# Two x batches and the later states transposed by DMA, a reordered dual phase, and a later softmax in an attention and maxout kernel

## Chip, cores and metric

One core of one Trainium2 chip. The metric is device time in microseconds (us) of one launch, lower is better. A run more than 1.5% above the fastest of the same kernel counts as slow. The kernel before takes 166.33 us (median of 4 runs, 166.04 to 167.13).

## The reference, cut

For each of 8 batches and 8 heads, x (512 x 64) and a state (32 x 64) read each other by softmax attention. The results are laid side by side into 4352 tokens of 512 features and go through a maxout layer and an output layer:

```python
scores = scale * x @ state.T;  xread = softmax(scores) @ state
scores2 = scale * state @ x.T; sread = softmax(scores2) @ x
x = concat([xread, sread], axis=2)          # -> (8 * 544, 512)
h = maximum(maximum(x @ w1, x @ w2), x @ w3)  # 512 -> 768
out = h @ w_out                              # 768 -> 512
```

## The kernel before

The kernel never forms xread. It folds the states into the weights once per batch (G = state times w1, w2, w3) and multiplies the transposed attention weights (aT) with G: "maxout" below, six matmuls of 512 columns for one of six column blocks, evacuated by one copy on ScalarE and two maxima on VectorE. The order of each engine's instructions is the program order. Batches 0 and 1 run together in a "dual phase"; from batch 2 on there is a loop, in which batch n = b + 1 is prepared in slots between the six maxouts of batch b.

```python
def load_x(b):                       # float32 in HBM -> bf16, cast by the DMA, GpSimd queue
    nc.gpsimd.dma_start(out=x_sb[b]..., in_=x[b]...)

def states(k, copy):                 # states of batches 2k, 2k+1
    p = pp.tile([128, 4, 128], BF16, tag="pw", bufs=4, name="pt")
    for t in range(4):
        nc.tensor.transpose(p[:, t, :], st[k][:, t]..., ident)
    for c in range(2):
        copy(out=bds[k][...], in_=p[...])

def x_transpose_dma(b):
    new(xT, b, [128, H, 2, 128], "xT")
    nc.sync.dma_start_transpose(out=xT[b]..., in_=x_sb[b][:, 0:XW])

def a_transpose_dma(b):
    new(aT, b, [128, J, 2, 128], "aT", bufs=3)
    nc.sync.dma_start_transpose(out=aT[b]..., in_=a[b]...)

# ... end of the dual phase, cut
    states(1, dve)
    x_transpose(2, 0, dve); x_transpose(2, 1, dve)      # on TensorE
    x_maxout(1, 3)
    g_cols(0, (5,), defer=both)
    scores(2, 0, 2); softmax(2, 0, 2, nc.gpsimd.tensor_mul)
    # ...
    a_transpose(2, 0, act); a_transpose(2, 1, dve)      # on TensorE
    ffn_out(0, 0); g_cols(2, (2, 3)); ffn_out(0, 1); g_cols(2, (4, 5))

for b in range(2, B):                                   # cut
    n = b + 1
    if n == 3: slots[0] += x_transpose(n, ...)          # on TensorE
    slots[0 or 1] += scores(n), softmax(n)
    slots[2] += a_transpose_dma(n)
    slots[3] += sread(n), states((n + 1) // 2, act)
    # G pieces in slots 1 (2 for n = 3), 4, 5; output pieces of batch b - 1 in slots 1, 2, 4, 5
```

The softmax here doesn't subtract the row's maximum and nothing guards it: scores larger than these inputs give would overflow.

## Time and profile before

| | before |
|---|---|
| median of 4 runs | 166.33 us |
| span of the profiled run | 164.5 us |
| TensorE busy | 149.7 us, 91% |
| ScalarE, VectorE, GpSimd busy | 60%, 58%, 27% |
| granted TensorE clock | 1.0 throughout |

TensorE is the engine to watch: it is on 63% of the chain of waits (the work followed back from the last instruction, at each step to what released it), and the others have slack over the whole. The prediction shows the lines and reads them.

### The profile page before, as it was taken

The numbers are of one execution on the slowest core, as the hardware profiler recorded it, in microseconds if no ns is written. First come the engines' busy times: TensorE is split into PE (matmuls) and PEld (weight loads), VectorE is DVE, ScalarE is ACT, GpSimd is POOL, SyncE is SP. The second block draws the span as 40 slices with busy tenths as digits, with TensorE's granted clock in tenths as the row PEclk, the third lists the DMA queues.
The fourth block names the chain that finished last, engine by engine and source line by source line (L and its number), as shares of the span: only waits on it lengthen the run. The fifth ranks groups of instructions, "written<-read, shape, count | busy, mean of one in ns | idle before, by whom it ended". The sixth has DMA issues, their size and how long they took to land.

```text
span 164.5 us, 3569 instructions
## 1 busy us (share of the span) xinstructions
PE 149.7 (91%) x1432; PEld 70.9 (43%) x1449; DVE 96.0 (58%) x162; ACT 99.1 (60%) x158; POOL 44.0 (27%) x64
## 2 busy tenths in 40 slices
PE   7658699988999999999999999999999999999990
PEld 2425243533445444434344434444444466665430
DVE  4675777889418553665548464865586455585001
ACT  3355578366896678853876688648755853333440
POOL 8975550106150601081016101410141010100140
PEclk9999999999999999999999999999999999999999
DMA  4999999800039999269992989460306030030373
GB/s 132 195 174 199 204 200 248 122 7 0 0 120 130 144 256 198 53 116 145 277 193 87 133 187 104 162 191 14 128 0 195 8 130 0 0 132 0 128 235 148
DMA packets 31824, 20.94 MB, mean 127 GB/s; under 512 B 17184, under 2 KB 29344, under 8 KB 31808
## 3 DMA queue, kind: packets, MB, share of 16 engines
q0 software_dynamic: 15632, 15.08, 46.3%
q1 hardware_dynamic: 16176, 5.64, 18.5%
q8 instruction: 11, 0.18, 0.5%
q14 instruction: 5, 0.04, 0.1%
HBM read 15.20 MB, written 8.91 MB: 147 GB/s over the span
## 4 chain that ended last, share of the span: by engine, by line
PE 63%; DVE 11%; ACT 10%; DMA 6%; POOL 4%; issue 4%; DVEq 0%; ACTq 0%; POOLq 0%
PE pw L260 34%; PE po L285 20%; DMA x<-in_x_dram 4%; PE pg L239 4%; DVE den L183 4%; DVE t L267 3%; ACT e L176 3%; ACT G L245 3%; DVE ht L268 3%; PE ps L171 2%; ACT t L264 2%; PE psr L216 2%; POOL w L94 1%; DMA out_dram<-osb 1%; POOL a L186 1%
## 5 line engine op out<-in xcount | busy, mean ns | idle before, releaser
L260 PE MATMUL pw<-aT,G 128*128 128x512 bf16 x288 | 71.2, 379 | 3.6 <-ACT G L245 1.8
L267 DVE TENSOR_TENSOR t<-t,pw 128x512 bf16<-128x512 bf16 (+1 forms) x54 | 35.1, 650 | 41.6 <-ACT t L264 40.0
L285 PE MATMUL po<-wout,ht 128*128 128x512 bf16 x188 | 47.9, 380 | 0.8
L260 PEld LDWEIGHTS <-G 128*128 128x128 bf16 x288 | 26.7, 98 | 36.2 <-issue 5.1
L245 ACT CAST G<-pg 128x768 bf16<-128x768 f32 x48 | 36.5, 805 | 8.0 <-PE pg L239 7.6
L264 ACT CAST t<-pw 128x512 bf16<-128x512 f32 (+1 forms) x54 | 30.5, 566 | 14.1 <-PE pw L260 12.6
L268 DVE TENSOR_TENSOR ht<-t,pw 128x512 bf16<-128x512 bf16 (+1 forms) x54 | 35.5, 658 | 5.6
L292 ACT COPY osb<-po 128x512 f32<-128x512 f32 x33 | 19.4, 587 | 21.2 <-PE po L285 20.7
L285 PEld LDWEIGHTS <-ht 128*128 128x128 bf16 x204 | 18.4, 98 | 23.6 <-issue 4.7
L301 POOL DMA_DIRECT2D out_dram<-osb x14 | 7.8, 559 | 70.2 <-ACT osb L292 70.2
L186 POOL TENSOR_TENSOR a<-e,rden 128x1024 bf16<-128x1024 bf16 (+1 forms) x8 | 14.4, 1800 | 33.4 <-DVE rden L185 19.8
L239 PE MATMUL pg<-w,bd 64*32 64x384 bf16 x384 | 13.0, 328 | 1.1 <-DMA w<-in_moe_w_dram 1.1
L183 DVE TENSOR_REDUCE den<-e 128x32 f32<-128x1024 bf16 (+1 forms) x9 | 9.9, 1095 | 2.6 <-ACT e L176 2.6
L176 ACT ACTIVATE e<-ps 128x1024 bf16<-128x1024 f32 x7 | 7.2, 1024 | 5.8 <-PE ps L171 5.8
L260 PE MATMUL pw<-ats,w 128*128 128x256 bf16 x72 | 8.8, 273 | 0.0
L239 PEld LDWEIGHTS <-bd 64*32 64x32 bf16 x384 | 3.6, 89 | 11.7 <-issue 11.7
L260 PEld LDWEIGHTS <-w 128*128 128x128 bf16 x72 | 7.0, 98 | 2.1
L94 POOL DMA_DIRECT2D w<-in_moe_w_dram x9 | 6.8, 770 | 0.0
L69 POOL DMA_DIRECT2D x<-in_x_dram x7 | 6.7, 957 | 0.0
L150 PE MATMUL pxt<-ident,x 128*128 128x128 bf16 x64 | 4.4, 219 | 2.2 <-DMA x<-in_x_dram 1.1
L134 ACT COPY bd<-pt 64x512 bf16<-64x512 bf16 x6 | 3.5, 580 | 4.2 <-PE pt L131 4.1
L171 PEld LDWEIGHTS <-xT 128*128 128x128 bf16 x128 | 4.7, 98 | 2.4 <-DVE xT L153 0.8
(42 smaller groups left out, 63.4 us busy)
## 6 DMA issues: line engine op xcount, KB each, us to landing
out_dram<-osb POOLq DMA_DIRECT2D x14, 512.0 KB, 3.7
x<-in_x_dram POOLq DMA_DIRECT2D x7, 512.0 KB, 9.0
w<-in_moe_w_dram POOLq DMA_DIRECT2D x3, 384.0 KB, 10.3
w<-in_moe_w_dram POOLq DMA_DIRECT2D x3, 256.0 KB, 8.2
wout<-in_moe_w_out_dram POOLq DMA_DIRECT2D x1, 768.0 KB, 16.4
x0f<-in_x_dram SPq DMA_DIRECT2D x1, 512.0 KB, 4.0
out_dram<-osb SPq DMA_DIRECT2D x1, 512.0 KB, 2.7
out_dram<-osb SPq DMA_DIRECT2D x2, 256.0 KB, 2.2
```

What stands on the lines that cost most here:

```text
L94: nc.gpsimd.dma_start(out=w_sb[c][:, :, i, :], in_=w.rearrange("(kk p) f -> p kk f", p=128)[:, :, m0 * 128:m1 * 128])
L176: nc.scalar.activation(out=e[b][:, :, g0:g1], in_=p, func=AF.Exp, scale=scale)
L183: nc.vector.reduce_sum(out=den, in_=e[b][:, :, g0:g1], axis=AX.X)
L186: mul(out=a[b][:, :, g0:g1].rearrange("p j g s n -> p j (g s) n"), in0=e[b][:, :, g0:g1].rearrange("p j g s n -> p j (g s) n"), in1=rden.r ...
L239: nc.tensor.matmul(p[32 * s:32 * s + 32, g, 0:384].rearrange("p (i f) -> p i f", i=3), bd(b, 2 * s + g)[64 * g:64 * g + 64, g, :], w[64 * ...
L245: copy(out=G[b][:, :, m * 384:(m + 1) * 384], in_=p[:, :, 0:384])
L260: nc.tensor.matmul(p[:, 0:n], lhs(i, k), rhs(k), start=(k == 0), stop=(k == nk - 1))
L264: nc.scalar.copy(out=t0[:, 0:n], in_=pw[0][:, 0:n])
L267: nc.vector.tensor_max(t1[:, 0:n], t0[:, 0:n], pw[1][:, 0:n])
L268: nc.vector.tensor_max(ht[b][:, m, :], t1[:, 0:n], pw[2][:, 0:n])
L285: nc.tensor.matmul(p, ht[b][:, m, j * 128:(j + 1) * 128], wout_sb[:, m, :], start=(m == 0), stop=(m == NM - 1))
L292: nc.scalar.copy(out=o[:, j, :], in_=p)
```

## The change

The intent: take transposes off TensorE (x of batches 2 and 3, states of groups 1 to 3, a of batch 2) and give them to the DMA; place states with GpSimd in place of ScalarE and VectorE; finish batch 0 (its last output pieces too) inside the dual phase, with the G pieces in pairs; move the loop's softmax behind the next maxima; split the last store. The diff, cut to its core:

```diff
 def states(k, copy):
-    p = pp.tile(...); 4 x nc.tensor.transpose(...)
+    if k == 0: (as before)
+    else:
+        p = data.tile([128, 4, 128], BF16, name=f"stT{k}")
+        nc.sync.dma_start_transpose(out=p, in_=st[k]...)
 ...
+    load_st(1, nc.scalar)
 ...
+    states_cast(1, pool)
     ... load_x(3)
+    states(1, pool)
+    x_transpose_dma(2)
 ...
-    x_maxout(1, 1); g_cols(0, (3, 4)); ...; x_maxout(1, 2); x_maxout(0, 3)
+    x_maxout(1, 1); x_maxout(1, 2); g_cols(0, (4, 5), defer=both)
+    x_maxout(0, 3); x_maxout(0, 4); g_cols(1, (3, 4), defer=both)
+    x_maxout(0, 5); x_maxout(1, 3)
     scores(2, 0, 2)
     softmax(2, 0, 2, nc.gpsimd.tensor_mul)
+    a_transpose_dma(2)
+    x_transpose_dma(3)
+    load_x(4)
 ...
+    ffn_out(0, 0) ... ffn_out(0, 3)     # all four output pieces of batch 0
 for b in range(2, B):
-    slots[0] softmax(n); slots[3] states(.., act); slots[4] g_cols(n, (2, 3))
+    slots[1] softmax(n); slots[2] states(.., pool); slots[3] g_cols(n, (2, 3))
 # last output piece: two tiles, stored on ScalarE's and SyncE's queues
-    act(o[:, j, 0:256]); dve(o[:, j, 256:512]); one store
+    act(halves[0]); store; dve(halves[1]); store
```

More of the change, by code (lines that the diff above doesn't have):

```diff
@@ L53 @@
     ctx.enter_context(tc.manual_schedule())
+    dve, act, pool = nc.vector.tensor_copy, nc.scalar.copy, nc.gpsimd.tensor_copy
     def load_st(k, eng):
@@ L127, in states @@
     def states(k, copy):
-        p = pp.tile([128, 4, 128], BF16, tag="pw", bufs=4, name="pt")
-        for t in range(4):
-            nc.tensor.transpose(p[:, t, :], st[k][:, t].rearrange("p c d -> p (c d)"), ident)
+        if k == 0:
+            p = pp.tile([128, 4, 128], BF16, tag="pw", bufs=4, name="pt")
+            for t in range(4):
+                nc.tensor.transpose(p[:, t, :], st[k][:, t].rearrange("p c d -> p (c d)"), ident)
+        else:
+            p = data.tile([128, 4, 128], BF16, name=f"stT{k}")
+            nc.sync.dma_start_transpose(out=p, in_=st[k].rearrange("p t c d -> p (t c d)"))
         for c in range(2):
@@ L288, in ffn_out @@
         if split:
-            nc.scalar.copy(out=o[:, j, 0:256], in_=p[:, 0:256])
-            nc.vector.tensor_copy(out=o[:, j, 256:512], in_=p[:, 256:512])
-        else:
-            nc.scalar.copy(out=o[:, j, :], in_=p)
+            halves = [work.tile([128, d_model // 2], F32, tag=f"oh{k}", bufs=1, name="oh") for k in range(2)]
+            rows = out[b * SP:b * SP + S, :].rearrange("(p j) f -> p j f", j=J)[:, j, :]
+            act(out=halves[0], in_=p[:, 0:256])
+            nc.scalar.dma_start(out=rows[:, 0:256], in_=halves[0])
+            dve(out=halves[1], in_=p[:, 256:512])
+            nc.sync.dma_start(out=rows[:, 256:512], in_=halves[1])
+            return
+        act(out=o[:, j, :], in_=p)
         if b == "s":
@@ L308, in late_transposes @@
             late.pop(0)()
-    dve, act, pool = nc.vector.tensor_copy, nc.scalar.copy, nc.gpsimd.tensor_copy
     both = (True, True)
@@ L331 @@
     a_transpose(0, 1, dve)
+    load_st(1, nc.scalar)
+    x_maxout(0, 0)
     x_transpose(1, 0, act)
     x_transpose(1, 1, dve)
-    x_maxout(0, 0)
+    sread(0)
     scores(1, 0, 2)
     softmax(1, 0, 2, nc.gpsimd.tensor_mul)
-    for k in range(1, B // 2):
+    states_cast(1, pool)
+    for k in range(2, B // 2):
         load_st(k, nc.gpsimd)
     load_x(3)
-    sread(0)
+    states(1, pool)
+    x_transpose_dma(2)
     g_cols(0, (1, 2))
@@ L346 @@
     x_maxout(0, 2)
+    x_maxout(1, 0)
     sread(1)
-    x_maxout(1, 0)
-    g_cols(1, (2,))
+    g_cols(1, (2,), (dve,))
+    g_cols(0, (3,), defer=both)
     x_maxout(1, 1)
-    g_cols(0, (3, 4), defer=(False, True))
-    states_cast(1, pool)
     x_maxout(1, 2)
+    g_cols(0, (4, 5), defer=both)
     x_maxout(0, 3)
+    x_maxout(0, 4)
     g_cols(1, (3, 4), defer=both)
-    x_maxout(0, 4)
-    states(1, dve)
-    x_transpose(2, 0, dve)
-    x_transpose(2, 1, dve)
+    x_maxout(0, 5)
     x_maxout(1, 3)
-    g_cols(0, (5,), defer=both)
     scores(2, 0, 2)
     softmax(2, 0, 2, nc.gpsimd.tensor_mul)
+    a_transpose_dma(2)
+    x_transpose_dma(3)
+    load_x(4)
+    for k in range(2, B // 2):
+        states_cast(k, pool)
     x_maxout(1, 4)
-    g_cols(1, (5,), defer=both)
-    states_cast(2, pool)
-    states_cast(3, pool)
-    x_maxout(0, 5)
+    g_cols(1, (5,))
+    g_cols(2, (0,))
+    ffn_out(0, 0)
+    x_maxout(1, 5)
     sread(2)
-    x_maxout(1, 5)
-    g_cols(2, (0, 1))
-    a_transpose(2, 0, act)
-    a_transpose(2, 1, dve)
-    ffn_out(0, 0)
-    g_cols(2, (2, 3))
+    g_cols(2, (1, 2))
     ffn_out(0, 1)
-    g_cols(2, (4, 5))
+    ffn_out(0, 2)
+    g_cols(2, (3, 4))
+    ffn_out(0, 3)
+    g_cols(2, (5,))
     assert not copies_due
-    pending = [(0, 2), (0, 3)] + [(1, j) for j in range(J)]
+    pending = [(1, j) for j in range(J)]
     for b in range(2, B):
@@ L385 @@
         if n < B:
-            if n == 3:
-                slots[0].append(lambda: x_transpose(n, 0, act))
-                slots[0].append(lambda: x_transpose(n, 1, dve))
-                slots[3].append(lambda: x_transpose_dma(n + 1))
-            elif n + 1 < B:
-                slots[0].append(lambda: x_transpose_dma(n + 1))
-            at = 1 if n == 3 else 0
-            slots[at].append(lambda: scores(n, 0, 2))
-            slots[at].append(lambda: softmax(n, 0, 2, nc.gpsimd.tensor_mul))
-            slots[2 if n == 3 else 1].append(lambda: g_cols(n, (0, 1)))
+            slots[0].append(lambda: scores(n, 0, 2))
+            slots[1].append(lambda: softmax(n, 0, 2, nc.gpsimd.tensor_mul))
+            slots[1].append(lambda: g_cols(n, (0, 1)))
             slots[2].append(lambda: a_transpose_dma(n))
             slots[3].append(lambda: sread(n))
-            slots[4].append(lambda: g_cols(n, (2, 3)))
+            slots[3].append(lambda: g_cols(n, (2, 3)))
             slots[5].append(lambda: g_cols(n, (4, 5)))
             slots[4].append(late_transposes)
+            if n + 1 < B:
+                slots[0].append(lambda: x_transpose_dma(n + 1))
             if n % 2 and n + 1 < B:
-                slots[3].append(lambda: states((n + 1) // 2, act))
-            for k in ((4, 5) if n == 3 else (n + 2,)):
-                if k < B:
-                    slots[0].append(lambda k=k: load_x(k))
+                slots[2].append(lambda: states((n + 1) // 2, pool))
+            if n + 2 < B:
+                slots[0].append(lambda: load_x(n + 2))
         else:
@@ L408 @@
                 slots[m].append(lambda m=m: s_maxout(m))
-        for m in (1, 2, 3, 4, 5) if len(pending) > 4 else (1, 2, 4, 5):
+        for m in (1, 2, 4, 5):
             if pending:
```

## The prediction

> **What bounds the kernel now.** I read the page first (shares, slices, chain of waits), then the chain in order of time, then the timeline and the waits of TensorE, then the DMA issues by stretch. The page:
>
> ```profile
> PE 149.7 (91%) x1432; PEld 70.9 (43%) x1449; DVE 96.0 (58%) x162; ACT 99.1 (60%) x158; POOL 44.0 (27%) x64
> PE   7658699988999999999999999999999999999990
> DMA  4999999800039999269992989460306030030373
> PE 63%; DVE 11%; ACT 10%; DMA 6%; POOL 4%; issue 4%; DVEq 0%; ACTq 0%; POOLq 0%
> ```
>
> TensorE is the bound: 91% busy, 63% of the chain. DMA is near full in slices 1 to 7, about 4 to 33 us. Busy flatters TensorE, because a matmul that waits in the pipeline counts as busy, so I count streaming. In the chain in order of time six matmuls of 512 columns last 1.29 us (215 ns each), so one piece of the second layer (six matmuls, "maxout" below) and one output piece (six, "po") cost 1.29 each. From the same view: G for one batch and two columns 0.45, scores 0.48, sread 0.56, sixteen x transposes 1.07, four state transposes 0.33, eight a transposes 0.5.
>
> Three places lose time. First, the dual phase (batches 0 and 1 together), here in the timeline of TensorE:
>
> ```profile
> 31.12 0.40 PE L131 MATMUL pt<-ident,st 128*128 128x128 bf16 x4
> 31.35 1.06 PE L150 MATMUL pxt<-ident,x 128*128 128x128 bf16 x16
> 32.55 0.59 PE L260 MATMUL pw<-aT,G 128*128 128x512 bf16 x2
> 33.81 1.02 PE L260 MATMUL pw<-aT,G 128*128 128x512 bf16 x4 [0.67 <-ACT t L264]
> 38.05 1.59 PE L260 MATMUL pw<-aT,G 128*128 128x512 bf16 x6 [0.78 <-ACT G L245]
> ```
>
> From 18.07 to 46.49 us TensorE has 24.5 us of streaming in 28.4: 3.9 lost, mostly after 31 us. The reader sees why: six matmuls that should take 1.29 stretch from 32.55 to 34.8, because VectorE is copying states and xT, and later ScalarE is late with G.
>
> Second, every batch of the later loop. The timeline of the loop of batch 5:
>
> ```profile
> 102.33 1.22 DVE L183 TENSOR_REDUCE den<-e 128x32 f32<-128x1024 bf16 x1 [0.29 <-ACT e L176]
> 103.92 0.63 DVE L267 TENSOR_TENSOR t<-t,pw 128x512 bf16<-128x512 bf16 x1
> 104.16 1.04 PE L260 MATMUL pw<-aT,G 128*128 128x512 bf16 x4
> 105.40 0.59 PE L260 MATMUL pw<-aT,G 128*128 128x512 bf16 x2 [0.20 <-DVE ht L268]
> 105.83 1.46 PE L285 MATMUL po<-wout,ht 128*128 128x512 bf16 x6
> ```
>
> The denominators stand ahead of the maxima, buffers come free late, and the six matmuls from 104.16 hold TensorE 1.67 us instead of 1.30: 0.37 lost per batch, of which only 0.20 shows as idle. A loop lasts 16.13 us (99.42 to 115.55 in the chain). Third, the end: ScalarE and VectorE copy the last piece one after the other, as the timeline shows, and only then a 256 KB store starts:
>
> ```profile
> 160.29 0.37 ACT L289 COPY osb<-po 128x256 f32<-128x256 f32 x1 [0.71 <-PE po L285]
> 160.70 0.42 DVE L290 COPY osb<-po 128x256 f32<-128x256 f32 x1 [8.63 <-DMA out_dram<-osb]
> ```
>
> The span ends at 164.5, 4.2 us after the last matmuls.
>
> **What the Trainium skill says.** "TensorE: Matmul & The Clock Gate", section Back-to-back issue gap, gives N/2.4 + 2.5 ns for an isolated warm matmul, 216 ns at 512 columns, and about 131 ns in a stream with weight loads. The trace has 215 ns in the stream; I use 215. "DMA: Bandwidth & Descriptors", section Issuing engines are not separate DMA queues, says that DMAs of all issuing engines interleave on the same 16 DMA engines; its section Queues, rings and completion order says that each engine takes turns between queue rows by packets. The trace agrees: a DMA transpose of a landed in 3.0 us at 106 us, with no x load near, and in 7.6 and 7.5 us at 72 and 89 us, when an x load was issued beside it. "GPSIMD Engine Reference", section 4.1 Engine selection, calls one-input operations on GpSimd roughly line rate; here the 128x512 state cast took 605 ns on GpSimd and 547 on VectorE, which agrees.
>
> **The change part by part.**
>
> Removed from TensorE: x transposes of batches 2 and 3 (2 x 1.07), state transposes of three groups (3 x 0.33), a transposes of batch 2 (0.5): 3.6 us. With them go, from ScalarE and VectorE, four xT copies (0.69 to 1.01), six state copies (about 0.6 each) and two aT copies. GpSimd gets the six state copies, in my estimate 0.6 to 0.8 us each from its cast; it is 27% busy.
>
> Early part, to 18 us: a batch 0 maxout goes ahead of the batch 1 transposes and fills a wait for x, but G then waits for the second weight chunk, which lands at 16.79 either way. The gain is lost there; scores of batch 1 come 0.4 later, so its a is ready 0.35 later. Net -0.35.
>
> Dual phase: summing the new order from 18.07: 11 maxouts 14.2, G 3.4, four po 5.2, a transposes 0.5, two sreads 1.1, scores 0.5: 24.9 us. With about 0.1 lost per pair of pieces (as in the good stretch 20.8 to 31.0 us) and the 0.35, TensorE could reach the first maxout of batch 2 at about 44.7. The old kernel gets there at 46.49 with two po (2.6) and the transposes of x3 (1.1) still to do: equal work at 50.2. So **5.5 us are to be had here, if the data come in time**.
>
> They will not quite. Batch 2's data now pass through a chain of DMAs that run when the queue is full:
>
> ```profile
> x<-in_x_dram POOLq DMA_DIRECT2D x7, 512.0 KB, 9.0
> ats<-sr SPq DMA_TRANSPOSE x8, 3.1
> aT<-a SPq DMA_TRANSPOSE x5, 4.2
> xT<-x SPq DMA_TRANSPOSE x4, 6.4
> ```
>
> x2 was issued at 12.82 and took 13.4 us: 26.2. Its DMA transpose takes 5.7 alone and 7.1 beside traffic; here w_out (until 30.1) and x3 (33.6) run beside it, so I put it at 8 to 9: about 35.3. TensorE reaches the scores of batch 2 at 33.7 (18.07 + 14.5 + 0.35 + 0.8). Waiting term 1: about 1.6. From the start of scores to the end of a took 5.46 us in the old dual phase (35.05 to 40.51). Then the transpose of a: 4.2, or 7.5 if the load of x4, which GpSimd issues right behind a, disturbs it. a lands at 35.3 + 5.5 + 4.2 to 7.5 = 45 to 48.3; I take 47.3 for the first maxout of batch 2, so waiting term 2 is about 1. The transpose of x3 stands behind that of a on the same queue, lands at 49 to 51, and scores of batch 3 are due one maxout later, at 48.6. Waiting term 3: about 1.3.
>
> Loop: the softmax moves one slot on, behind the next maxima. Walking batch 5 with it, each PSUM buffer comes free before it is needed, so I take back 0.37 of 16.13: 15.76 for a loop with four po. State transposes (0.33 in two of the loops) go. Five loops: 78.8.
>
> The last batch and the last seven po: unchanged, 131.68 to 160.29 = 28.6. End: both halves are copied at once and stored on two queues, 0.6 sooner: 3.6.
>
> **Sum:** 47.3 + 1.3 + 78.8 + 28.6 + 3.6 = 159.6 of span. The measured time is 2.1 over the span (166.61 against 164.5), so **161.7 us**, 3% faster.
>
> **Rivals.** *No wait worth naming*: x2 lands early enough and x4 does not disturb a. For it: a transpose of a took 4.2 at 56 us beside an output store. Against it: full DMA slices until 33 us. It takes terms 1 to 3 away: about 158. *The wait takes the gain*: the state transpose goes first on the queue and GpSimd, which must copy the states, stands behind DMA issues; scores of batch 2 come at 37 or later, and all behind it shifts. For it: state loads took 10 us in the old kernel. Against it: the load of group 1 now goes on ScalarE's hardware queue at 12 us. About 164 to 165. *ScalarE becomes the bound in the dual phase*: 14 G copies (0.80), 11 t copies (0.6), e, aT and four osb copies make 22.4 us against TensorE's 24.9, and ahead of the loop it has some 10 us of work for 9.9 of TensorE's. It can cost 1 us, but hides behind the wait for a: 162. In the loop, the *state transposes* stand behind that of a with GpSimd's copies after them, some 12 us after the softmax slot, when the next scores need them at 13.5: at worst 1 us in two loops.
>
> **Range and chances.** All terms at their good end give 158, waiting 3 us longer 165. I take 158.5 to 165.0. The 2% line is 163.3; terms 1 to 3 would have to grow by 1.6 together, which I give one chance in four. Slower needs over 8 us of new waits: 0.02.
>
> **What would show it.** After: no pt past group 0, no pxt past batch 1; chain from about 33 to 49 us through DMA xT, a on GpSimd and DMA aT; TensorE waits on DMA of 2 to 5 us in all, at scores of batch 2, first maxout of batch 2 and scores of batch 3; loops of 15.7 to 15.8; end 3.6 after the last matmul. Wrong if those waits exceed 6 us or are absent, if loops stay at 16.1, or if a wait on GpSimd's state copies appears at scores of batches 4 and 6.

## The result, and the profile after

The changed kernel takes **176.24 us** (median of 4 fast runs, 175.22 to 176.51). Ratios here are the mean time of one kernel's fast runs over that of the other's of the same rounds, so not quite the ratio of the medians quoted; it is 1.058 (95% interval 1.052 to 1.064). The prediction was 161.7, faster. The kernel is 6% slower.

The page of the profile after, the lines that answer to those of before, with the row of the granted clock:

```profile
PE 149.2 (86%) x1381; PEld 69.1 (40%) x1397; DVE 93.4 (54%) x157; ACT 94.5 (54%) x151; POOL 49.8 (29%) x69
...
PE   7777689889930089999999999999999999999990
...
PEclk9999999999996557999999999999999999999998
DMA  4999999940999992549978769924230702030264
...
PE 66%; DMA 18%; DVE 7%; ACT 3%; POOL 2%; issue 1%; SPq 0%; DVEq 0%; POOLq 0%; ACTq 0%
```

Every slice but a few looks as good as before. There is one hole of two slices (some 52 to 61 us) in which no compute engine works and the DMA engines do, and the clock row drops to half there. The DMA share of the chain is up from 6% to 18%.

The chain of waits in order of time (start, length, what), after:

```profile
27.09 9.83 DMA xT<-x
36.97 0.65 PE ps L176 x16
...
43.89 17.76 DMA xT<-x
61.69 1.03 PE ps L176 x16
62.72 2.56 PE pw L265 x6
65.28 0.77 PE pg L244 x15
...
80.13 0.47 PE ps L176 x16
...
95.83 0.47 PE ps L176 x16
```

The transpose of x3 (43.89) takes 17.76 us, and the scores of batch 3 (61.69) wait for it. After it the same work runs at half speed: scores 1.03 for 0.48, six matmuls 2.56 for 1.29. From 80.13 on a loop takes 15.70 us, where it took 16.13 before. TensorE's waits after (total, times, longest), the first three:

```profile
PE ps L176 <- DMA xT<-x: 10.6, 1, 10.6
PE pw L265 <- DVE t L272: 1.5, 3, 0.5
PE pw L265 <- DMA aT<-a: 1.5, 1, 1.5
```

What else is in flight? Two lines of the timeline after (start, length of the issue):

```profile
42.41 0.95 POOL L70 DMA_DIRECT2D x<-in_x_dram  x1
42.48 1.23 SPq L207 DMA_TRANSPOSE aT<-a  x1
```

and the list of DMA issues after, for 42.4 to 44.2 us (size, us from issue to landing):

```profile
x<-in_x_dram POOLq DMA_DIRECT2D x1, 512.0 KB, 9.2
aT<-a SPq DMA_TRANSPOSE x1, 7.1
...
xT<-x SPq DMA_TRANSPOSE x1, 17.8
```

GpSimd issues the load of x4 in the moment in which SyncE issues the transpose of a; the transpose of x3 follows 1.4 us later on the same queue. The two stores of batch 0 are issued at 45.7 and 48.9, the load of x5 at 49.4. The DMA queues between 46 and 47 us, after (q0 is GpSimd's queue, q1 SyncE's; packets, MB, share of 16 engines):

```profile
q0 software_dynamic: 274, 0.14, 115.7%
q1 hardware_dynamic: 3, 0.00, 0.4%
```

The transposes get 3 packets of 277. (A share above 100% means that packets overlap in time.) What these three are shows in the same view for 43 to 46 us and then for 46 to 48 us, SyncE's queue alone:

```profile
q1 hardware_dynamic: 1024, 0.26, 50.7%
...
q1 hardware_dynamic: 24, 0.00, 1.6%
```

The transpose of a is 256 KB, 1024 packets of 256 bytes, so all its data had moved by 46 us, in about the time that it takes alone. What came late are the small packets that close it (4 bytes each in the packed trace): they trickle out until 49.4 beside the load, and the first data packets of x3 move only from 48 us on. In e1, e3, e5, e9 and e10 too the queue stands after exactly 1024 packets. So "starved" below is not a count of turns lost packet by packet: the queue stood at the end of a, with x3 behind it.

### The profile page after: what moved, and what is told of

Same layout as the page of the kernel before. It is cut to its first block, busy times and chain, and to the rows that moved or that the text cites. A ratio compares the mean times of both kernels' runs of the same rounds, so it can differ in the third digit from the quotient of the medians.

```text
span 174.4 us, 3476 instructions
## 1 busy us (share of the span) xinstructions
PE 149.2 (86%) x1381; PEld 69.1 (40%) x1397; DVE 93.4 (54%) x157; ACT 94.5 (54%) x151; POOL 49.8 (29%) x69
## 4 chain that ended last, share of the span: by engine, by line
PE 66%; DMA 18%; DVE 7%; ACT 3%; POOL 2%; issue 1%; SPq 0%; DVEq 0%; POOLq 0%; ACTq 0%
PE pw L265 33%; PE po L290 23%; DMA xT<-x 16%; PE pg L244 4%; DMA x0f<-in_x_dram 2%; PE ps L176 2%; PE psr L221 2%; DVE den L188 2%; POOL a L191 2%; ACT e L181 2%; DVE ht L273 1%; DVE t L272 1%; DVE xT L158 1%; ACT t L269 1%; PE pat L202 1%
## 5 line engine op out<-in xcount | busy, mean ns | idle before, releaser
L265 PE MATMUL pw<-aT,G 128*128 128x512 bf16 x288 | 72.1, 385 | 4.3 <-DVE t L272 1.5
L290 PE MATMUL po<-wout,ht 128*128 128x512 bf16 x189 | 48.2, 382 | 1.0 <-issue 0.2
L250 ACT CAST G<-pg 128x768 bf16<-128x768 f32 x47 | 35.8, 803 | 12.2 <-PE pg L244 11.9
L290 PEld LDWEIGHTS <-ht 128*128 128x128 bf16 x204 | 19.0, 98 | 25.0 <-issue 5.2
L191 POOL TENSOR_TENSOR a<-e,rden 128x1024 bf16<-128x1024 bf16 (+1 forms) x8 | 14.4, 1799 | 48.9 <-DVE rden L190 39.6
L310 POOL DMA_DIRECT2D out_dram<-osb x14 | 7.9, 562 | 49.6 <-ACT osb L301 49.5
L181 ACT ACTIVATE e<-ps 128x1024 bf16<-128x1024 f32 x7 | 7.2, 1024 | 16.3 <-PE ps L176 16.3
L176 PE MATMUL ps<-bd,xT 128*128 128x64 bf16 x112 | 5.0, 200 | 10.9 <-DMA xT<-x 10.6
L139 POOL COPY bd<-stT 64x512 bf16<-64x512 bf16 x6 | 6.4, 1067 | 16.8 <-DMA stT<-st 16.6
```

Source lines behind the costliest of these rows:

```text
L176: nc.tensor.matmul(p[:, 2 * jj:2 * jj + 2, g - g0, s, :], xT[b][:, h, jj, :], bd(b, h).rearrange("p c n -> p (c n)"), start=(g == g0 and s ...
L181: nc.scalar.activation(out=e[b][:, :, g0:g1], in_=p, func=AF.Exp, scale=scale)
L191: mul(out=a[b][:, :, g0:g1].rearrange("p j g s n -> p j (g s) n"), in0=e[b][:, :, g0:g1].rearrange("p j g s n -> p j (g s) n"), in1=rden.r ...
L250: copy(out=G[b][:, :, m * 384:(m + 1) * 384], in_=p[:, :, 0:384])
L265: nc.tensor.matmul(p[:, 0:n], lhs(i, k), rhs(k), start=(k == 0), stop=(k == nk - 1))
L290: nc.tensor.matmul(p, ht[b][:, m, j * 128:(j + 1) * 128], wout_sb[:, m, :], start=(m == 0), stop=(m == NM - 1))
```

## The experiments

The first eight ran on one chip (kernel before: 165.87 to 165.98 median), the last four on another, which is less steady (four of the eleven runs of before were slow there; its fast ones took 165.66 to 168.01). So ratios are compared.

| run | median us | ratio to before (95%) | a of batch 2, issue to landing | x3, issue to landing |
|---|---|---|---|---|
| the change | 176.24 | 1.058 (1.052 to 1.064) | 7.1 | 17.8 |
| e1_xT3_first | 165.27 | 0.994 (0.986 to 1.001) | 7.4 | early |
| e2_x4_late | 163.10 | 0.980 (0.970 to 0.990) | 3.2 | 4.3 |
| e3_xT4_late | 174.87 | 1.050 (1.041 to 1.059) | 7.6 | 16.6 |
| e4_x3_on_PE | 165.28 | 0.996 (0.989 to 1.004) | 7.3 | on TensorE |
| e5_x5_late | 177.42 | 1.067 (1.059 to 1.074) | 7.1 | 16.3 |
| e6_keep_busy | 175.57 | 1.055 (1.046 to 1.064) | 7.3 | 18.1 |
| e7_x3_late | 163.59 | 0.976 (0.967 to 0.985) | 3.3 | 4.3 |
| e8_singles | 164.44 | 0.989 (0.983 to 0.996) | 3.2 | 4.3 |
| e9_stores_late | 168.77 | 1.015 (1.007 to 1.023) | 7.3 | 9.5 |
| e10_x4_no_cast | 175.41 | 1.050 (1.041 to 1.058) | 8.7 | 17.6 |
| e11_softmax_slot0 | 169.61 | 1.016 (1.011 to 1.022) | 3.2 | 4.3 |
| e12_states_early | 164.44 | 0.981 (0.974 to 0.989) | 3.2 | 4.3 |

All twelve gave correct results. Some medians include one or two slow runs, the ratios do not; the profile of e7 and that of e10 fell into the slow state, so no times of TensorE are drawn from these two; their DMA times are given, and nothing rests on them alone.

**My theory after the result:** the transposes of a and x3 are starved by ordinary traffic on the other queue, above all by the x4 load. **Rivals:** two big transposes in a row are slow in any company; the transpose of x4, queued behind, takes the engines; the stores or the x5 load do it; the cast in the load does it.

### e1_xT3_first: the transpose of x3 ahead of the traffic

```diff
     x_transpose_dma(2)
+    x_transpose_dma(3)
 ...
     a_transpose_dma(2)
-    x_transpose_dma(3)
     load_x(4)
```

> The changed kernel with one line moved: the DMA transpose of x3 is issued right behind that of x2, ahead of that of a of batch 2, so before the load of x4 (42.4 us) and the stores of batch 0 begin. Theory (traffic): the 10.6 us wait at the scores of batch 3 comes from the transpose of x3 being in flight beside the x4 load and the stores; early, it lands by about 42, the wait is gone and with it the low clock behind it: 176.2 - 10.6 - 2.4 = about 163. Rival (two big transposes in a row are slow whatever runs beside them): it lands 10 us or more after that of x2, about 47 to 55, and the scores of batch 2 or the transpose of a are delayed instead: 168 or more.

165.27. The transpose of x3 is done long before it is needed, the wait at the scores of batch 3 is gone, and only the wait for a of batch 2 remains (1.7 us, 1.5 in the changed kernel). The expected 163 was missed by 2: this profiled run lost 3.2 us waiting for weights early on (1.3 in the changed kernel), an early DMA wait that differs from run to run. Two transposes in a row are not slow as such.

### e2_x4_late: the x4 load out of the way

```diff
     x_transpose_dma(3)
-    load_x(4)
 ...
+            if n == 3:
+                slots[0].append(lambda: load_x(4))
             slots[0].append(lambda: scores(n, 0, 2))
```

> The changed kernel with the load of x4 issued in the loop of batch 2 instead of right behind a of batch 2. If the x4 load is what holds the transposes: a lands in about 4.2 us instead of 7.1 and x3 in 6 to 8 instead of 17.8, the scores of batch 3 start near 51, and the time is about 164 to 167 (the transpose of x4 then comes later and may delay a of batch 3). If the stores of batch 0 or the x5 load hold them, x3 still lands after 58 and the time stays at 174 or more.

163.10, under the lower end that I expected, and 2% under the kernel before. The same view of the queues between 46 and 47 us in e2, which has no line for q0:

```profile
q1 hardware_dynamic: 834, 0.21, 114.0%
```

and the DMA issues of a and x3 in e2:

```profile
aT<-a SPq DMA_TRANSPOSE x1, 3.2
...
xT<-x SPq DMA_TRANSPOSE x1, 4.3
```

834 packets in a microsecond against 3. The store of batch 0, issued at 46.24, moves its first packets at 48, when the transposes are nearly done (x3 lands at 48.7). So this run does not show what a store does beside a transpose.

### e3_xT4_late and e5_x5_late: two other suspects

```diff
-                slots[0].append(lambda: x_transpose_dma(n + 1))
+                slots[3 if n == 3 else 0].append(lambda: x_transpose_dma(n + 1))   # e3
-                slots[0].append(lambda: load_x(n + 2))
+                slots[3 if n == 3 else 0].append(lambda: load_x(n + 2))            # e5
```

> The changed kernel with the DMA transpose of x4 moved from slot 0 to slot 3 of the loop of batch 2, so that it is no longer queued 7 us behind that of x3. If the transpose of x4 takes the engines from that of x3 (both in flight 51.7 to 61.7): x3 lands near 53 to 55 and the time falls to about 167 to 169. If loads and stores do it: x3 lands near 60 as before, 174 to 177.

> The changed kernel with the load of x5 moved from slot 0 to slot 3 of the loop of batch 2 (it was issued at 49.4, so in flight for the last 12 us of the transpose of x3). If the x4 load alone does the damage: x3 still lands at 60 or later, 174 to 176. If each x load holds the transposes while it is in flight: x3 lands 2 to 4 us after x4 has landed, at 54 to 56, and the time is 167 to 170.

174.87 and 177.42; x3 still needs 16.6 and 16.3 us. Neither the transpose of x4 nor the x5 load is needed for the wait. In e5 I had expected x3 to land soon after x4 if loads do the harm; it landed at 63.0, some 9 us after x4. So something else carried on after the x4 load: the stores were left.

### e9_stores_late: the stores of batch 0 held back as well

```diff
 # on top of e5
-            nc.gpsimd.dma_start(out=out[b * SP:...], in_=o[...])      # for b == 0
+            held.append(store) if b == 0 else store()
 ...
+            if n == 3:
+                slots[3].insert(0, lambda: [held.pop(0)() for _ in range(2)])
```

> The kernel with the x5 load late (177.4, x3 landing 16.3 us after issue), and the two stores of batch 0 also held back until after the scores of batch 3. The x4 load is then the only traffic beside the transposes of a and x3. If the x4 load only blocks them while it is in flight (to about 9 us after issue) and the stores do the rest: x3 lands some 2 to 4 us after x4, 10 to 12 us after its own issue, and the time is 168 to 171. If the stores have no part in it: still 15 us or more, 175 to 177.

168.77 (ratio 1.015 against 1.067 for e5), and x3 lands in 9.5 us, about 2 us after x4. Between 46 and 47 us in e9:

```profile
q0 software_dynamic: 305, 0.16, 125.9%
q1 hardware_dynamic: 10, 0.00, 1.4%
```

So the x4 load alone holds x3 until about the time it has landed (9 of the 17 us), and the stores that are queued behind it account for the other 7 (16.3 in e5, 9.5 here). What a store does to x3 with no load ahead of it, no run tests; the nearest thing is a transpose of a in the kernel before, beside the tail of an x load and a store (56 us), which took 4.2 us against 3.0 alone.

### e10_x4_no_cast: is it the cast?

```diff
-    load_x(4)
+    x4_f = data.tile([128, XW], F32, name="x4f")
+    nc.gpsimd.dma_start(out=x4_f..., in_=x[4]...)        # float32, no cast
 ...
+            if n == 3:
+                slots[0].append(lambda: pool(out=x_sb[4][:, 0:XW], in_=x4_f))
```

> The changed kernel with x4 loaded at the same place on the same queue, but as float32 into a tile of its own, without the cast during the DMA; GpSimd casts it later (about 2.4 us). If it is the casting load (packets of 512 B) that starves the transposes: a lands in 3 to 5 us, x3 in 5 to 8, no long wait, 163 to 167. If any load of 512 KB issued at that moment does it: a in 7 us and x3 in 15 or more, 174 to 178.

175.41; a takes 8.7 and x3 17.6 us. The cast is not the cause. (The load is listed with 1024 KB here, as it writes float32.)

### e4_x3_on_PE: one part undone

```diff
     a_transpose_dma(2)
-    x_transpose_dma(3)
     load_x(4)
 ...
+            if n == 3:
+                slots[0].append(lambda: x_transpose(n, 0, act))
+                slots[0].append(lambda: x_transpose(n, 1, dve))
             slots[0].append(lambda: scores(n, 0, 2))
```

> The changed kernel with only x3 transposed on TensorE again, at the start of the loop of batch 2, as in the kernel before; x2 stays on the DMA and the x4 load stays beside the transpose of a. If the starved transpose of x3 is the whole cause of the slowdown: the 10.6 us wait and the low clock go, 1.07 of transposes and a copy come back: 176.2 - 10.6 - 2.5 + 1.5 to 3 = 165 to 166.5. If the changed order of the dual phase or the softmax slot were to blame too, it stays above 168.

165.28, as expected of x3 as the whole cause: with x3 alone back on TensorE the change is even with the kernel before. The transposes of x2 and a by DMA, the order of the dual phase, and the softmax slot do not make it slow.

### e6_keep_busy: the low clock

```diff
+            if n == 3:
+                slots[0].append(lambda: keep_busy(46))     # 46 matmuls of zeros
             slots[0].append(lambda: scores(n, 0, 2))
```

> The changed kernel with 46 matmuls of zeros (about 9.9 us) on TensorE just before the scores of batch 3, so that TensorE is busy while it would wait. The wait for the transpose stays. The low clock after it (0.5 to 0.6 from 54 to 66 us) should be gone if idleness caused it: 1.03 to 0.48 for the scores, 2.56 to 1.29 for the next six matmuls, 0.3 for G, about 0.6 for po, in all some 2.4 us: about 173.8. If the clock is low for another reason the time stays at 176.

The whole time, 175.57, hardly differs. The stretch in question does; two lines of e6's timeline of TensorE:

```profile
63.30 0.64 PE L176 MATMUL ps<-bd,xT 128*128 128x64 bf16 x16 [0.74 <-DMA xT<-x]
...
79.02 0.63 PE L176 MATMUL ps<-bd,xT 128*128 128x64 bf16 x16
```

From the scores of batch 3 to those of batch 4 it takes 15.7 us where the changed kernel took 18.4, so 2.7 us were the clock. Most of that does not show at the end: this profiled run came to the scores of batch 3 later by 1.6 us (63.30 against 61.69; a of batch 2 was already issued 1.3 us later, after 2.1 us of waiting for weights early on, against 1.3), and it waited 0.3 us for another a later. That accounts for 1.9 of the 2.2 us by which its span missed the gain; the rest is open. Over the runs the gain is within the noise (1.055 against 1.058). The clock itself, in the table of stretches (start:end, length, then busy us of TensorE, weight loads, VectorE, ScalarE, GpSimd, then granted clock, DMA share, GB/s), changed kernel:

```profile
50.00:52.00 2.00, 1.14 (x6) 0.29 (x3) 0.97 (x2) 0.59 (x1) 0.32 (x1) 1.00 0.68 76
52.00:54.00 2.00, 0.00 (x0) 0.00 (x0) 0.41 (x1) 0.00 (x0) 0.00 (x0) 0.88 1.20 95
54.00:56.00 2.00, 0.00 (x0) 0.00 (x0) 0.00 (x0) 0.00 (x0) 0.00 (x0) 0.50 1.29 112
...
64.00:66.00 2.00, 2.00 (x21) 0.32 (x19) 1.36 (x3) 0.51 (x2) 0.00 (x0) 0.50 1.35 197
66.00:68.00 2.00, 1.78 (x14) 0.81 (x8) 1.50 (x3) 1.31 (x2) 0.25 (x1) 0.70 0.11 10
```

In e6 the clock is 1.00 from 52 to 80 us. The Trainium skill, "TensorE: Matmul & The Clock Gate", section What's actually happening, says that idleness of some 3.4 us halves the clock and that as much sustained work restores it. The trace agrees on the half (0.50) but not on the times: in finer stretches of the same view the clock fell at about 53.5, 2.4 us after the last matmul ended, and was restored at about 67.2, 5.5 us after matmuls began again (61.7).

### e7_x3_late and e8_singles: what is left of the dual phase

```diff
 # e7, on top of e2
-    load_x(3)
     states(1, pool)
+    load_x(3)
 # e8, on top of e7: one G piece between two maxouts
-    g_cols(0, (3,), ..); x_maxout(1, 1); x_maxout(1, 2); g_cols(0, (4, 5), ..); x_maxout(0, 3); x_maxout(0, 4); ...
+    x_maxout(1, 1); g_cols(0, (3,), ..); x_maxout(1, 2); g_cols(0, (4,), ..); x_maxout(0, 3); g_cols(0, (5,), ..); ...
```

> The kernel with the x4 load late (163.1), and the load of x3 also moved, behind the two GpSimd copies of the states (about 32 us), so that it is not in flight while x2 is transposed (27.5 to 37.1, 9.6 us). If loads hold transposes: x2 in 5 to 7 us, landing at 33 to 35. The time falls only if TensorE is at the scores of batch 2 before 37: by my reading it is not, so 162 to 163.3. If the transpose of x2 is held by the w_out load instead, it still takes 9 us or more.

> As the previous run, with the G pieces of the dual phase one at a time between single maxouts, in place of pairs between pairs of maxouts. If two maxouts in a row run out of PSUM buffers (three waits of TensorE for VectorE of 0.5 us, one for G of 0.8): these waits go and TensorE reaches the first maxout of batch 2 some 2 us earlier: 160.5 to 161.5. If ScalarE is the bound of that stretch, nothing changes: 162 to 163.

In e7 the transpose of x2 takes 7.1 us in place of 9.6 (7.2 in e8), so the x3 load holds it as the x4 load holds the others; 163.59, even with e2 as expected. e8 is a miss: 164.44, not 161. It did bring TensorE to the first maxout of batch 2 at 47.51 (48.69 in e2), less than the 2 us I expected, and then gave it all back; TensorE's waits in e8:

```profile
PE ps L176 <- POOL bd L139: 2.1, 1, 2.1
PE pw L265 <- DVE t L272: 1.4, 5, 0.5
```

The scores of batch 4 started at 66.80, in e2 at 66.43: they stand behind GpSimd's state copies, which stand behind the DMA transposes of x4, a and the states on one queue. And the waits for VectorE are still 1.4 us in all, so pairs of maxouts were not their only cause.

### e12_states_early: that wait taken away

```diff
 # on top of e8, in the dual phase behind x_transpose_dma(3)
+    for k in range(2, B // 2):
+        states_dma(k)           # the DMA part of states(k); GpSimd's copies stay where they were
```

> As the run with single G pieces and the x3 load late (164.4), with the DMA transposes of the states of groups 2 and 3 issued right behind that of x3 in the dual phase, in place of behind that of a of batches 3 and 5. There TensorE waited 2.1 us for GpSimd's state copies at the scores of batch 4. If that wait was the gain of the single pieces given back: it goes, scores of batch 4 start at 64.6 instead of 66.8, 162 to 162.5. If another wait stands just behind it (the transpose of x4 or of a of batch 3): 163.5 to 164.5.

The wait for GpSimd is gone and another stands in its place:

```profile
PE pw L271 <- DMA aT<-a: 1.7, 1, 1.7
```

It is a of batch 3, behind the transpose of x4 on the queue. Its four fast runs took 162.6 to 164.8; the ratio 0.981 is that of e2 within the intervals. So e2, e7 and e12 are all some 2% better than the kernel before, and these runs do not rank them.

### e11_softmax_slot0: the later softmax

```diff
 # on top of e2
-            slots[1].append(lambda: softmax(n, 0, 2, nc.gpsimd.tensor_mul))
+            slots[0].append(lambda: softmax(n, 0, 2, nc.gpsimd.tensor_mul))
```

> The kernel with the x4 load late (163.1), with the softmax of the loop put back into slot 0, ahead of the maxima of the second maxout, as in the kernel before. If the later softmax is what makes the loops shorter (15.7 against 16.1): loops of 16.05 to 16.1, five times 0.37 = 1.8 more, 164.6 to 165.2. If the other moves in the loop (G pieces, loads, states off TensorE) do it: loops stay at 15.7 and the time within 0.5 of 163.1.

169.61, ratio 1.016 against 0.980: the later softmax is worth more than the 1.8 us that I had reckoned. The scores in the chain of e11 in order of time:

```profile
69.45 0.64 PE ps L176 x16
...
85.69 0.47 PE ps L176 x16
...
103.89 0.64 PE ps L176 x16
...
120.12 0.48 PE ps L176 x16
```

and TensorE's first two waits in e11:

```profile
PE ps L176 <- POOL bd L139: 3.2, 2, 2.1
PE pw L265 <- DMA aT<-a: 2.0, 1, 2.0
```

Undisturbed loops take 16.24 and 16.23 us, 0.5 more than the 15.7 of e2: the direct cost, a little more than I had read off. One loop takes 18.2, because putting the softmax into slot 0 also puts GpSimd's a ahead of its x load in program order, so that each load is issued right behind a and beside the transposes of a and the states. Those of a took 8.0 and 7.4 us at 75 and 91 us, and that of the states at 92 us 9.3. It is the accident of batch 3 again, in small.

## Why the prediction was wrong

The prediction's own sign came up: waits of TensorE on transposes by DMA of 12.1 us, where it had said 2 to 5, and wrong above 6. Term by term, from the sum of the prediction (span) to the measured 174.4:

| step | predicted | measured | difference |
|---|---|---|---|
| first maxout of batch 2 starts (waiting terms 1 and 2 included) | 47.3 | 49.7 | +2.4 |
| waiting term 3, scores of batch 3 on x3 | 1.3 | 10.6 | +9.3 |
| low clock after it | not in the sum | 2.7 (18.4 for a loop of 15.7) | +2.7 |
| a loop | 15.76 | 15.70 | -0.3 in five |
| last batch and last seven po | 28.6 | 28.6 (141.66 to 170.25) | 0 |
| end | 3.6 | 4.1 | +0.5 |

The differences add to 14.6 us, and 159.6 + 14.6 is the measured span to 0.2.

**The step that failed is waiting term 3:** "The transpose of x3 stands behind that of a on the same queue, lands at 49 to 51". It landed at 61.7: 12 us after a (49.6), where the prediction left 3 to 4. It had read in the trace that an x load beside a transpose of a more than doubles it, and applied that to a alone; x3 behind it was taken to run as if nothing flowed, but was held by the load and then by the stores, which term 3 does not count. (Nor do turns by packets, to which the prediction puts the doubling, fit the trace: in the kernel before, too, all 1024 data packets of the a issued at 72 us had moved by 75.5, and only its closing packets came late.) e2 shows what the step takes undisturbed: with the x4 load elsewhere a lands in 3.2 and x3 in 4.3 us. (The 5.7 that the prediction took for a transpose of x alone was not the least: that at 68.09 us in the kernel before took 4.3.) e9 shows the split of the 17: about 9 with the load alone, about 7 more with the stores behind it. e4 shows that this one transpose is the whole loss against the kernel before.

**A cost was missing:** an engine that stands still for long comes back slower. 2.7 us of the loss, shown by e6 in the stretch, though not in the whole time.

**Mis-sized: the dual phase.** I let TensorE reach the first maxout of batch 2 at 44.7 without waits for data; it was ready at about 48.2 (the last G piece starts at 47.83, and the wait for a then shows as 1.48). The 0.1 us lost per pair of pieces was too low. Two of the three places that lose 0.5, in the timeline of TensorE after:

```profile
31.11 1.47 PE L265 MATMUL pw<-aT,G 128*128 128x512 bf16 x6 [0.52 <-DVE t L272]
...
35.36 1.47 PE L265 MATMUL pw<-aT,G 128*128 128x512 bf16 x6 [0.52 <-DVE t L272]
```

So the change's real gain in TensorE's order up to there is some 2 us, not 5.5. e8 reached that maxout 1.2 us sooner than e2 (two single profiles); the rest stays open.

**Right: the loop and its reason.** 0.37 per loop was predicted, 0.43 measured, and e11 shows that the softmax slot does it. **Right in kind: waiting term 2.** The step from scores to the end of a took 5.5 us as predicted (36.97 to 42.46), and a landed 7.1 later, near the upper end that I gave. Waiting term 1 (1.6) hardly showed: x2 landed at 36.9 (predicted 35.3), but TensorE came to the scores of batch 2 only then, 3 us after the 33.7 predicted, and its list of waits has none for x2.

**Wrong: the end.** The halves were to be copied at once. VectorE's copy still starts when ScalarE's ends; the timeline after:

```profile
170.28 0.37 ACT L296 COPY oh<-po 128x256 f32<-128x256 f32 x1 [0.71 <-PE po L290]
170.68 0.42 DVE L298 COPY oh<-po 128x256 f32<-128x256 f32 x1 [8.63 <-ACT oh L296]
```

In the program that is built, VectorE's copy carries a wait for ScalarE, although the two write different tiles; they read one PSUM tile. Taking the output tile apart was not enough.

**GpSimd's state copies** take 1067 ns, not my 600 to 800, as this group (count, busy us, mean ns, idle before) of the page after shows; it cost nothing in the changed kernel, but waits appear on it in e2 (0.6), e8 and e11, where the rival in the prediction had put them:

```profile
L139 POOL COPY bd<-stT 64x512 bf16<-64x512 bf16 x6 | 6.4, 1067 | 16.8 <-DMA stT<-st 16.6
```

What stays open: why the closing packets of a come so late beside a load, why x3's packets then stay few beside the stores (in e9, without stores, they are few until 50.5 too), and whether stores with no load ahead of them would do the same.

## What to carry to other kernels

A transpose moved from TensorE to the DMA is not free when other things flow: the same one took 4 us alone and 16 to 18 beside one 512 KB load and two stores, so place loads by what is on the transpose queue in that moment, not only by when their own data are needed. When the trace shows that a load slows one transfer, charge that to every transfer queued behind it for as long as the load lasts. And a wait of ten microseconds cost more than ten here: TensorE came back at half clock for 5.5 us, which was worth 2.7.

## What the Trainium skill lacked or had wrong

- "DMA: Bandwidth & Descriptors", section Rules for kernel authors, says of a transpose next to ordinary DMAs that it "needs nothing". For the result that held in all thirteen kernels; for time it did not: in the fast profiles a took 3.2 alone against 7.1 to 7.6 us beside the load, x3 4.3 against 16.3 to 18.1 with stores behind it. A line on this cost is lacking.
- "TensorE: Matmul & The Clock Gate", section Back-to-back issue gap: some 131 ns for a 512-column matmul in a stream. All profiles here have 215 ns (six in 1.29 us), the figure that it gives for an isolated one.
- "GPSIMD Engine Reference", section 4.1 Engine selection: one-input operations roughly at line rate. True of the 128x512 cast (605 ns against 547 on VectorE), not of the permuting 64x512 copy: 1067 ns against 580 on ScalarE and 686 on VectorE in the kernel before (those two read PSUM, GpSimd reads SBUF, so part of it may be the source).
